# An opening with sums apart from products, and loads held back behind marks, in a fused window-attention and feed-forward kernel

## The chip, the cores and the metric

The kernel runs on one core of one Trainium2 chip. The metric is the device time of one execution in microseconds (us), as a median of runs. Nothing else runs on the chip.

## The reference

Eight batches, eight heads, 576 tokens, head dimension 64. Each token attends to the tokens at most 32 positions away. The attention's output, heads side by side, goes through a feed-forward layer with a leaky ReLU. Inputs and output are float32.

```python
scores = q @ k.T / sqrt(64)                       # per batch and head
scores = where(abs(pos_q - pos_k) <= 32, scores, -1e9)
attn = softmax(scores)
x = (attn @ v), heads side by side                # 4608 tokens x 512
h = x @ w_in                                      # 512 -> 2048
g = maximum(0.01 * h, h)
out = g @ w_out                                   # 2048 -> 512
```

## The kernel before

**Units of work.** Heads go in pairs: head p and head p + 4 lie on partitions 0 to 63 and 64 to 127, so there are four pairs p. Attention is cut into 64 steps: step i is batch i // 8, half (i // 4) % 2 of its 576 tokens (288 tokens), pair i % 4. The feed-forward layer is cut into 16 halves g of 288 tokens; half g needs the four steps 4g to 4g + 3. Each half has 16 tiles `h_tile(g, f)` (128 of the 2048 hidden units, four matmuls over the 512 inputs, one for each pair c, in one PSUM bank). The output is cut into 36 tiles of 128 tokens (`o_tile`, 16 matmuls, one copy on ScalarE (ACT), one store issued from ACT's queue).

**One attention step.** `score(i)`: five matmuls of keys (block-diagonal `kbd`) against `qT` into `ps` (L242), the exponential `e` on ACT (L248), the product with a 0/1 mask on GpSimd (POOL) into `pr` (L252). `weighted(i)`: on TensorE (PE) the sums `s` (ones times `pr`, L276 and L279, or one matmul L274 where VectorE (DVE) has joined the two parts beforehand, from step 12 on), then the products `x` with the values `vbd` (L286); on DVE the reciprocal `r` of `s` (L292) and the product of `x` and `r` into `xT` (L294). `ps`, `x` and `s` have one PSUM buffer each. `xT` is what `h_tile` reads.

**Getting q, k and v in place.** SyncE (SP) issues the float32 loads (`load_qk`, `load_v`). `cast_qk` turns q and k to bf16, on POOL, or q on DVE where `nc.vector` is given. Batches 0 to 2 are then transposed by PE (`transposes`, L201, six small matmuls for one q or k into a bank of the pool `mmps`, four banks that `h_tile` and `o_tile` also use) and copied out by ACT (L209, L215); batches 3 to 7 (`BY_DMA = 3`) by DMA transposes that SP issues (`transpose_dma`, L187), after which ACT copies as well. `place_keys` puts keys into `kbd` on DVE (L227). `cast_v` puts values into `vbd`, on POOL, or on ACT for pairs 1 to 3 of batch 0.

**Order.** Everything is ordered by hand; each engine runs its instructions in the order in which the program issues them. The opening (L427 to L488) does batch 0 and the feed-forward halves 0 and 1: step by step `score(i + 1)`, some idle matmuls (`keep_busy`, which multiply the mask and are read by nobody), `weighted(i)`; after the first four steps the 16 tiles of g = 0 with steps 5 to 7 between them; then the 16 tiles of g = 1, with the transposes of batch 1 after every fourth tile. `step()` does one later step: `score(i + 2)`, `weighted(i)`, and casts, transposes and loads for the batches to come by the table `PLAN`. From L493 on a list of `h_tile` and `o_tile` pieces is walked with a planned clock, and `spend` calls `step()` when a step's due time has come; the output tiles of half g = 1 come first.

**Loads.** The weights are loaded and cast by DMAs that POOL issues, w_in in four chunks of two DMAs each (`load_w_in`, L412; one per head row a), w_out in four chunks (`load_w_out`, L418). A load can be held back by a *mark*: a DMA of one element, from a tile that is written late into the buffer that is to be loaded, issued first (L70, L81). Batch 1's q and k stand behind a mark on w_in's second chunk (L459), its v behind a mark on w_out's second chunk (L473). Batch 2's q and k are issued without a mark, one pair before each of the steps 8 to 11 (L524).

Of the kernel before, what the change touches and what calls it, by code (L numbers as in the profile page):

```python
# [16 lines left out]
def kernel(  # L17
# [12 lines left out]
    nc = tc.nc  # L30
# [18 lines left out]
    cast = ctx.enter_context(tc.tile_pool(name="cast", bufs=1))  # L49
    attn = ctx.enter_context(tc.tile_pool(name="attn", bufs=2))  # L50
    kt = ctx.enter_context(tc.tile_pool(name="kt", bufs=4))
    prob = ctx.enter_context(tc.tile_pool(name="prob", bufs=4))
    tdma = ctx.enter_context(tc.tile_pool(name="tdma", bufs=1))
    outp = ctx.enter_context(tc.tile_pool(name="outp", bufs=4))
    PS = bass.MemoryType.PSUM
# [68 lines left out]
    nc.vector.memset(kbd[0], 0.0)  # L124
    clear(vbd[0], 0)
    clear(vbd[0], 1)

# [8 lines left out]
    for lo in (0, 64):  # L138
        w = win[lo:lo + 64]
        nc.gpsimd.affine_select(  # L140
            out=w, in_=w, compare_op=ALU.is_ge, fill=0.0,
            base=0, channel_multiplier=-1, pattern=[[0, 3], [1, 128]],
        )
        nc.gpsimd.affine_select(
            out=w, in_=w, compare_op=ALU.is_ge, fill=0.0,
            base=2 * W, channel_multiplier=1, pattern=[[0, 3], [-1, 128]],
        )
    win_f = win.rearrange("p n c -> p (n c)")
    mask = [const.tile([128, NCOL], BF16, name=f"mask{i}") for i in range(2)]

# [27 lines left out]
                nc.gpsimd.tensor_copy(out=vbd[b % 2][r, p, :, r], in_=vf[b, p][r])  # L178


    BY_DMA = 3
    qkT, asked = {}, {}

    def transpose_dma(b, p):
        for which, src in (("q", qb), ("k", kb)):
            t = tdma.tile([128, RUN, 96], BF16, name=f"{which}T{p}")
            nc.sync.dma_start_transpose(out=t, in_=src[:, p].rearrange("p c a d -> p (c a d)"))  # L187
            qkT[b, p, which] = t
        asked[b, p] = state["done"]

    def transposes(b):

# [44 lines left out]
    def score(i):  # L237
        b, hf, p = where(i)
        ps = scps.tile([128, 1024], FP32, name="ps")
        c0 = 512 - HALF  # L240
        for blk, q0, n in WIN[hf]:
            nc.tensor.matmul(  # L242
                ps[:, c0:c0 + n], kbd[b % 2][:, p, blk],
                qT[b][:, p, q0:q0 + n], start=True, stop=True,
            )
            c0 += n
        e = attn.tile([128, NCOL], BF16, name="e")
        nc.scalar.activation(  # L248
            out=e, in_=ps[:, 512 - HALF:512 - HALF + NCOL], func=AF.Exp, scale=scale,
        )  # L250
        pr = prob.tile([128, NCOL], BF16, name="pr")
        nc.gpsimd.tensor_mul(pr, e, mask[hf])  # L252
        probs[i] = pr, None

    def join(i):


        hf = where(i)[1]
        pr = probs[i][0]
        both = prob.tile([128, HALF], BF16, name="both")  # L260
        o0 = ODD[hf]
        o1 = o0 + NCOL - HALF
        nc.vector.tensor_add(both[:, o0:o1], pr[:, o0:o1], pr[:, HALF:NCOL])  # L263
        rest = slice(0, o0) if o0 else slice(o1, HALF)
        nc.vector.tensor_copy(out=both[:, rest], in_=pr[:, rest])  # L265
        probs[i] = pr, both

    def weighted(i):
        b, hf, p = where(i)
        pr, both = probs.pop(i)  # L270
        x = xps.tile([128, HALF], FP32, name="x")
        s = xps.tile([128, HALF], FP32, name="s")
        if both is not None:
            nc.tensor.matmul(s, ones_bd, both, start=True, stop=True)  # L274
        else:
            nc.tensor.matmul(  # L276
                s, ones_bd, pr[:, 0:HALF], start=True, stop=False, skip_group_check=True,
            )
            nc.tensor.matmul(  # L279
                s[:, ODD[hf]:ODD[hf] + NCOL - HALF], ones_bd, pr[:, HALF:NCOL],  # L280
                start=False, stop=True, skip_group_check=True,
            )
        c0 = 0
        for n_, (blk, q0, n) in enumerate(WIN[hf]):
            a = q0 - HALF * hf
            nc.tensor.matmul(  # L286
                x[:, a:a + n], vbd[b % 2][:, p, blk, :], pr[:, c0:c0 + n],
                start=(n_ == 0), stop=(n_ == len(WIN[hf]) - 1), skip_group_check=True,
            )
            c0 += n  # L290
        r = attn.tile([128, HALF], FP32, name="r")
        nc.vector.reciprocal(r, s)  # L292
        t0 = (b * S + hf * HALF) % RING
        nc.vector.tensor_mul(xT[:, p, t0:t0 + HALF], x, r)  # L294

    gT = const.tile([128, FFC, RING], BF16)

    def h_tile(g, f):  # L300

        t0 = g * HALF % RING
        h = mmps.tile([128, 512], FP32, name="mm", tag="mm")
        for c in range(DMC):
            nc.tensor.matmul(  # L305
                h[:, 0:HALF], w_in_bf[:, c, ts(f, 128)], xT[:, c, ds(t0, HALF)],
                start=(c == 0), stop=(c == DMC - 1),
            )
        nc.scalar.activation(  # L309
            out=gT[:, f, ds(t0, HALF)], in_=h[:, 0:HALF], func=AF.Prelu, alpha=0.01,  # L310
        )

    def o_tile(j, hook=None):

# [46 lines left out]
    def step():  # L361
# [7 lines left out]
        if b > 0:  # L369
            upto = 8 * (b + 1) + (PLAN[b > 1][0][r] if b + 1 < BY_DMA else 0)  # L370
            step_transposes(max(upto - 1, 8 * (b + 1)))
        if i < 7:
            score(i + 1)
        elif 8 <= i < NC - 2:
            nb, _, np_ = where(i + 2)
            if nb >= BY_DMA:
                step_transposes(8 * nb + 2 * np_ + 2)
                place_keys()
            score(i + 2)
# [2 lines left out]
        if b > 0:  # L382
            step_transposes(upto)
        if 0 < b < B - 1:
            for p in PLAN[b > 1][1][r] if b + 1 <= BY_DMA else ():
                cast_qk(b + 1, p)
                if b + 1 == BY_DMA:
                    transpose_dma(b + 1, p)
                if b + 2 < B:
                    load_qk(b + 2, p)  # L390

            n, p = (b + 1, 3) if r == 0 else (b + 2, r - 4)
            if p in range(4 if r == 0 else 3) and BY_DMA < n < B:
                step_transposes(8 * (n - 1) + 2 * p + 2)
                place_keys()
                cast_qk(n, p)
                transpose_dma(n, p)
                if n + 1 < B:
                    load_qk(n + 1, p)
# [7 lines left out]
    w_in_r = moe_w_in.rearrange("(a u d) f -> a d u f", a=2, d=D)  # L407
    w_out_r = moe_w_out.rearrange("(c p) f -> p c f", p=128)

    def load_w_in(f0, f1):  # L410
        for a in range(2):
            nc.gpsimd.dma_start(  # L412
                out=w_in_bf[64 * a:64 * a + 64, :, f0:f1], in_=w_in_r[a, :, :, f0:f1],
            )
# [14 lines left out]
    cast_qk(0, 1, nc.vector)  # L429
    first_pair()  # L430
    first_pair()
    clear(vbd[0], 2)
    cast_v(0, 0)
    cast_qk(0, 2, nc.vector)
    score(0)
    load_w_in(0, 512)
    first_pair()
    clear(vbd[0], 3)
    cast_qk(0, 3, nc.vector)
    load_w_in(512, 1024)  # L440
    for i in range(NPAIR):
        score(i + 1)
        if i + 1 < NPAIR:
            cast_v(0, i + 1, on_act=True)
        if i < 2:
            load_w_in(1024 + 512 * i, 1536 + 512 * i)
        else:
            load_w_out(i - 2)
        if i > 0:
            keep_busy(3 if i == 1 else 2)  # L450
        weighted(i)
        if i == 0:
            first_pair()
    state["done"] = NPAIR

    for p in range(NPAIR):
        load_qk(1, p, w_in_bf[0:1, 0, 512:514] if p == 0 else None)  # L459
    keep_busy(2)  # L460
    step()
    load_w_out(2)
    load_w_out(3)
    for f in range(FFC):
        h_tile(0, f)
        if f in (2, 6, 10):
            step()
        if f % 4 == 3:
            nc.gpsimd.memset(kbd[1][:, f // 4], 0.0)
    cast_qk(1, 0, nc.vector)  # L470
    cast_qk(1, 1, nc.vector)
    for p in range(NPAIR):
        load_v(1, p, w_out_bf[0:1, 4, 0:2] if p == 0 else None)  # L473
    second = transposes(1)
    for f in range(FFC):
        h_tile(1, f)
        if f % 4 == 3:
            p = f // 4
            next(second)
            next(second)  # L480
            place_keys()
            if p + 2 < NPAIR:
                cast_qk(1, p + 2, nc.vector)
            nc.gpsimd.memset(vbd[1][:, p], 0.0)  # L484
        if f == 11:
            score(8)
    state["tp"] = 16
    score(9)  # L488

# [11 lines left out]
    for us, kind, g, f in plan:  # L503
        if kind == "h" and f == 0:
            at[g] = t
        t += us
    due = []
    for i in range(8, NC):
        prev = 0.9 * O_US * 4 if i < 12 else at[i // 4 - 1] - LEAD
        due.append(prev + (at[i // 4] - LEAD + (1.2 if i < 12 else 0) - prev) * (i % 4 + 1) / 4)  # L510
    clock = 0.0
    cast_v(1, 0)
    turn = 0

    def spend(us):
        nonlocal clock, turn
        while due and due[0] <= clock:
            due.pop(0)
            i = state["done"]
            if i < 11:  # L520
                cast_v(1, i - 7)

            if i < 12:
                load_qk(2, i - 8)  # L524
            step()
            if 10 <= i < 14:
                load_v(2, i - 10)

        b, p = state["tp"] // 8, state["tp"] % 8 // 2
        turn += 1  # L530
        if kind == "o" and turn % 2 and b >= BY_DMA and (b, p, "k") in qkT and state["done"] > asked[b, p] + 2:
            step_transposes(state["tp"] + 1)
            place_keys()
        clock += us
# [35 lines left out]
```

## Time and profile before

| what | value |
|---|---|
| median of 3 runs | 328.59 us (328.4 to 329.43) |
| the profiled execution | 329.43 us, span 327.72 us |
| PE busy | 305.5 us, 2463 matmuls |
| DVE busy | 225.9 us |
| ACT busy | 223.6 us |
| POOL busy | 180.3 us |
| DMA transposes issued by SP | 40 |
| HBM read, written | 36.70 MB, 9.44 MB |
| granted TensorE clock | 1.0 |

The profile is of one execution. Busy times are of the span, which starts with the first instruction that the profiler holds and ends with the last; the time of the execution is 1.71 us longer. A busy PE is one with a matmul in flight, and matmuls overlap, so group means of matmuls are longer than their spacing. In lines of the timeline the columns are start, duration (both us), engine, line of the kernel, operation, what it writes and reads, and in brackets how long the engine was idle before and who released it; "SPq" and "ACTq" are those engines' queues when they issue a DMA. In a line of stages the columns are the stage, its length, and busy time with the number of instructions for PE, weight loads (PEld), DVE, ACT and POOL, then the granted clock, the DMA engines' mean share (transfers in flight on one engine can overlap, so it can exceed 1) and GB/s. In lines of DMA queues the columns are packets, MB and the time that the packets took as a share of the sixteen DMA engines' time.

### The profile page before, as it was taken

Reading aid. Unit: us, or ns where it says so; the run is one execution under the profiler, and the core shown is the slowest. Engines: PE = TensorE matmul, PEld = TensorE weight load, DVE = VectorE, ACT = ScalarE, POOL = GpSimd, SP = SyncE. Lnnn points to the kernel's source line nnn. Section 1 sums busy time; section 2 is a strip of 40 time slices with the busy share of each in tenths; the row PEclk is TensorE's granted clock in tenths of the full one; section 3 lists DMA queues with packets and bytes.
Section 4 is the critical chain, followed back from the end, with each engine's and each line's share of the span. In section 5 each row is a group of like instructions: output and inputs, shape, how many; then the busy total and the mean of one; then the engine's idle time right before and its main releaser. Section 6 shows DMA issues by size and latency. Waiting matters only on the chain.

```text
span 327.7 us, 6571 instructions
## 1 busy us (share of the span) xinstructions
PE 305.5 (93%) x2463; PEld 205.2 (63%) x2485; DVE 225.9 (69%) x310; ACT 223.6 (68%) x432; POOL 180.3 (55%) x213
## 2 busy tenths in 40 slices
PE   2578999689999999999999999999999999999996
PEld 1446784358585675758585666667675767666653
DVE  5489744587874997779776988689758867565200
ACT  6775791349385898878787878878786656555541
POOL 7798747566775596519841597339642545131000
PEclk9999999999999999999999999999999999999999
DMA  8999979968999999945997199916831001010102
GB/s 187 223 200 206 269 187 207 241 156 190 239 171 198 228 173 238 218 137 128 203 236 131 66 167 245 226 71 92 185 80 65 34 12 55 0 66 0 67 11 85
DMA packets 85172, 48.28 MB, mean 147 GB/s; under 512 B 64020, under 2 KB 80660, under 8 KB 85140
## 3 DMA queue, kind: packets, MB, share of 16 engines
q1 hardware_dynamic: 75524, 34.22, 55.6%
q10 hardware_dynamic: 5328, 9.44, 8.5%
q0 software_dynamic: 4288, 4.20, 7.9%
q8 instruction: 19, 0.31, 0.4%
q14 instruction: 13, 0.11, 0.1%
HBM read 36.70 MB, written 9.44 MB: 141 GB/s over the span
## 4 chain that ended last, share of the span: by engine, by line
PE 78%; DMA 10%; DVE 3%; POOL 3%; SPq 2%; issue 2%; ACT 1%; ACTq 0%; DVEq 0%; POOLq 0%
PE mm L305 34%; PE mm L322 33%; DMA kf<-in_k_dram 10%; PE x L286 4%; PE ps L242 4%; DVE r L292 2%; PE s L274 2%; SPq L72 1%; SPq L83 1%; POOL pr L252 1%; POOL vbd L484 1%; PE tp L201 1%; DVE xT L294 1%; POOL kb L168 1%; POOL vbd L178 0%
## 5 line engine op out<-in xcount | busy, mean ns | idle before, releaser
L292 DVE RECIPROCAL r<-s 128x288 f32<-128x288 f32 x64 | 125.1, 1954 | 35.7 <-PE s L274 26.1
L252 POOL TENSOR_TENSOR pr<-e,mask 128x544 bf16<-128x544 bf16 x64 | 77.9, 1218 | 103.2 <-ACT e L248 83.3
L305 PE MATMUL mm<-xT,w_in_bf 128*128 128x288 bf16 x1024 | 133.1, 286 | 0.0
L322 PE MATMUL mm<-w_out_bf,gT 128*128 128x512 bf16 (+2 forms) x571 | 128.3, 373 | 1.1
L309 ACT ACTIVATE gT<-mm 128x288 bf16<-128x288 f32 x256 | 101.3, 414 | 22.1 <-PE mm L305 9.4
L305 PEld LDWEIGHTS <-w_in_bf 128*128 128x128 bf16 x1024 | 98.3, 98 | 23.9
L322 PEld LDWEIGHTS <-gT 128*128 128x128 bf16 x592 | 56.4, 98 | 59.8
L248 ACT ACTIVATE e<-ps 128x544 bf16<-128x544 f32 x64 | 40.0, 624 | 26.3 <-ACT o_sb L327 5.7
L327 ACT ACTIVATE o_sb<-mm 128x512 f32<-128x512 f32 (+2 forms) x37 | 21.7, 586 | 45.8 <-PE mm L322 45.8
L227 DVE COPY kbd<-kT 64x576 bf16<-64x576 bf16 x64 | 28.6, 447 | 28.8 <-ACT kT L215 28.2
L178 POOL CAST vbd<-vf 64x576 bf16<-64x576 f32 x58 | 38.7, 668 | 1.9
L294 DVE TENSOR_TENSOR xT<-x,r 128x288 bf16<-128x288 f32 x64 | 29.3, 458 | 6.7
L168 POOL CAST kb<-kf 96x768 bf16<-96x768 f32 x32 | 27.3, 854 | 9.8 <-DMA kf<-in_k_dram 9.8
L242 PE MATMUL ps<-qT,kbd 128*128 128x128 bf16 (+2 forms) x320 | 26.8, 216 | 3.1 <-ACT e L248 3.1
L242 PEld LDWEIGHTS <-kbd 128*128 128x128 bf16 x320 | 20.9, 101 | 11.6 <-issue 3.6
L286 PE MATMUL x<-pr,vbd 128*128 128x128 bf16 (+2 forms) x320 | 26.3, 214 | 1.8 <-DVE xT L294 1.3
L263 DVE TENSOR_TENSOR both<-pr 128x256 bf16<-128x256 bf16 x52 | 23.5, 452 | 3.4 <-POOL pr L252 2.5
L286 PEld LDWEIGHTS <-vbd 128*128 128x128 bf16 x320 | 20.8, 99 | 6.6 <-DVE xT L294 2.1
L209 ACT ACTIVATE qT<-qT 128x576 bf16<-128x576 bf16 x20 | 23.6, 1179 | 1.2 <-ACT o_sb L327 1.2
L215 ACT ACTIVATE kT<-kT 128x576 bf16<-128x576 bf16 x20 | 23.5, 1177 | 0.0
L265 DVE COPY both<-pr 128x32 bf16<-128x32 bf16 x52 | 21.1, 405 | 0.0
L168 POOL CAST qb<-qf 96x768 bf16<-96x768 f32 x24 | 19.7, 821 | 0.0
(39 smaller groups left out, 110.2 us busy)
## 6 DMA issues: line engine op xcount, KB each, us to landing
qf<-in_q_dram SPq DMA_DIRECT2D x32, 288.0 KB, 4.7
kf<-in_k_dram SPq DMA_DIRECT2D x32, 288.0 KB, 5.4
vf<-in_v_dram SPq DMA_DIRECT2D x64, 144.0 KB, 5.1
out_dram<-o_sb ACTq DMA_DIRECT2D x35, 256.0 KB, 2.1
w_in_bf<-in_moe_w_in_dram POOLq DMA_DIRECT2D x8, 256.0 KB, 6.4
w_out_bf<-in_moe_w_out_dram POOLq DMA_DIRECT2D x4, 512.0 KB, 14.0
qT<-qb SPq DMA_TRANSPOSE x20, 4.9
kT<-kb SPq DMA_TRANSPOSE x20, 4.2
```

Of the source, the lines that this page charges most:

```text
L168: eng.tensor_copy(out=dst[:, p], in_=src[b, p].rearrange("p a (c d) -> p c a d", d=D),)
L178: nc.gpsimd.tensor_copy(out=vbd[b % 2][r, p, :, r], in_=vf[b, p][r])
L227: nc.vector.tensor_copy(out=kbd[b % 2][r, p, :, r], in_=kT[r].rearrange("p (n j) -> p n j", j=64),)
L242: nc.tensor.matmul(ps[:, c0:c0 + n], kbd[b % 2][:, p, blk], qT[b][:, p, q0:q0 + n], start=True, stop=True,)
L248: nc.scalar.activation(out=e, in_=ps[:, 512 - HALF:512 - HALF + NCOL], func=AF.Exp, scale=scale,)
L252: nc.gpsimd.tensor_mul(pr, e, mask[hf])
L286: nc.tensor.matmul(x[:, a:a + n], vbd[b % 2][:, p, blk, :], pr[:, c0:c0 + n], start=(n_ == 0), stop=(n_ == len(WIN[hf]) - 1), skip_group_c ...
L292: nc.vector.reciprocal(r, s)
L294: nc.vector.tensor_mul(xT[:, p, t0:t0 + HALF], x, r)
L305: nc.tensor.matmul(h[:, 0:HALF], w_in_bf[:, c, ts(f, 128)], xT[:, c, ds(t0, HALF)], start=(c == 0), stop=(c == DMC - 1),)
L309: nc.scalar.activation(out=gT[:, f, ds(t0, HALF)], in_=h[:, 0:HALF], func=AF.Prelu, alpha=0.01,)
L322: nc.tensor.matmul(o[:, lo:hi], gT[:, f, ds(128 * j % RING, 128)], w_out_bf[:, f, lo:hi], start=(f == 0), stop=(f == FFC - 1),)
```

## The change

- `weighted` is split into `sums` (matmuls into `s`, and the reciprocal), `product` (matmuls into `x`) and `scaled` (the product into `xT`). In the opening they are issued apart: a step's sums may come before the transposes of another pair, its product after. `keep_busy` is no longer called.
- `h_first(g, hooks)` issues the first four tiles of a half pair by pair over four PSUM banks: for each pair c, the matmuls of the four tiles. For g = 0 attention work stands as hooks before the pairs c = 2 and c = 3.
- The first chunk of w_in is issued one head row at a time; the order of casts, clears and weight loads in the opening is another.
- Batch 1's q and k stand behind a mark on w_out's first chunk; its v follows without a mark. Three of the four transposes of batch 1's pairs, and the scores of steps 8 and 9, move from half g = 1 into the output tiles that follow it, with due times of their own.
- Each of batch 2's loads stands behind a mark on the `xT` that the step before it has written.
- `BY_DMA = 4`: batch 3 is transposed by PE, batches 4 to 7 by DMA.

```diff
-    prob = ctx.enter_context(tc.tile_pool(name="prob", bufs=4))
+    prob = ctx.enter_context(tc.tile_pool(name="prob", bufs=6))
+    joined = ctx.enter_context(tc.tile_pool(name="joined", bufs=2))
+    recip = ctx.enter_context(tc.tile_pool(name="recip", bufs=3))
...
+    clear(vbd[0], 2)
...
+    nc.gpsimd.memset(vbd[0][:, 3], 0.0)
...
-    BY_DMA = 3
+    BY_DMA = 4
...
+    def h_first(g, hooks):
+        hs = [mmps.tile([128, 512], FP32, name="mm", tag="mm") for _ in range(4)]
         for c in range(DMC):
+            if c in hooks:
+                hooks[c]()
+            for f in range(4):
+                h_mms(g, f, hs[f], (c,))
+        for f in range(4):
+            h_out(g, f, hs[f])
...
     first_pair()
     first_pair()
     cast_v(0, 0)
+    score(0)
     cast_qk(0, 2, nc.vector)
+    score(1)
+    load_w_in(0, 512, (0,))
+    next(first)
+    sums(0)
+    next(first)
+    product(0)
+    place_keys()
     cast_qk(0, 3, nc.vector)
+    scaled(0)
+    sums(1)
+    cast_v(0, 1, on_act=True)
+    score(2)
+    load_w_in(0, 512, (1,))
     load_w_in(512, 1024)
+    next(first)
+    next(first)
+    place_keys()
+    product(1)
+    scaled(1)
+    cast_v(0, 2, on_act=True)
+    load_w_in(1024, 1536)
+    sums(2)
+    score(3)
+    load_w_in(1536, 2048)
+
+    def before_2():
+        product(2)
+        scaled(2)
+        cast_v(0, 3, on_act=True)
+        sums(3)
+        score(4)
+        load_w_out(0)
+
+    def before_3():
+        product(3)
+        scaled(3)
+        sums(4)
+        score(5)
+        load_w_out(1)
+
+    state["done"] = NPAIR
+
+    def second_half():
+        i = state["done"]
         weighted(i)
+        if i < 7:
+            sums(i + 1)
+        if i < 6:
+            score(i + 2)
+        state["done"] += 1
+
+    h_first(0, {2: before_2, 3: before_3})
     load_w_out(2)
     load_w_out(3)
+    for p in range(NPAIR):
+        load_qk(1, p, w_out_bf[0:1, 0, 0:2] if p == 0 else None)
+    for p in range(NPAIR):
+        load_v(1, p)
+    second_half()
+    for f in range(4, FFC):
         h_tile(0, f)
+        if f in (7, 11):
+            second_half()
...
     cast_qk(1, 0, nc.vector)
     cast_qk(1, 1, nc.vector)
     second = transposes(1)
...
+    second_half()
+    h_first(1, {})
+    for f in range(4, FFC):
         h_tile(1, f)
+        if f == 13:
+            second_pair(0)
...
+    due = [
+        (0.0, lambda: score(8)), (1.0, lambda: second_pair(1)), (2.6, lambda: second_pair(2)),
+        (3.2, lambda: score(9)), (4.4, lambda: second_pair(3)),
+    ]
+    due += [(6.0 + 1.9 * n, step) for n in range(NPAIR)]
...
+            step()
+            mark = place(i)[0:1, 0:2]
             if i < 12:
-                load_qk(2, i - 8)
-            step()
+                load_qk(2, i - 8, mark)
             if 10 <= i < 14:
-                load_v(2, i - 10)
+                load_v(2, i - 10, mark)
```

## The prediction

> **What bounds the kernel now.** I read the page first, for who is busy and where; then the busy table by stages, for where PE is not; then the chain and the timeline of the bad stages; then the DMA view of short windows, because the DMA engines turn out to set the opening. The page's busy line and slices:
>
> ```profile
> PE 305.5 (93%) x2463; PEld 205.2 (63%) x2485; DVE 225.9 (69%) x310; ACT 223.6 (68%) x432; POOL 180.3 (55%) x213
> ...
> PE   2578999689999999999999999999999999999996
> ...
> DMA  8999979968999999945997199916831001010102
> ```
>
> PE is the bound, except in the first nine slices of 8.2 us, where DMA is full. The stages say how much is missing:
>
> ```profile
> 0.00:20.00 20.00, 9.62 (x79) 6.76 (x81) 10.85 (x21) 14.54 (x20) 15.34 (x29) 1.00 1.09 203
> 20.00:48.00 28.00, 25.23 (x256) 19.19 (x254) 21.64 (x24) 20.20 (x47) 20.31 (x23) 1.00 1.09 219
> 48.00:71.00 23.00, 18.19 (x127) 9.50 (x127) 11.93 (x13) 7.11 (x13) 15.03 (x17) 1.00 1.03 214
> 71.00:324.00 253.00, 251.77 (x2001) 169.25 (x2020) 181.52 (x254) 181.18 (x354) 129.58 (x146) 1.00 0.64 130
> ```
>
> The second figure is PE's. From 71 us on only 1.2 us are idle in 253, so every PE instruction added there is paid in full and nothing removed elsewhere there gains. Idle before: 10.4 us up to 20, 2.8 up to 48, 4.8 up to 71 (while g = 1's output tiles run). The timeline shows what costs the last 4.8 us: output stores that wait on ACT's queue with the next exponentials behind them.
>
> ```profile
> 56.62 0.37 ACTq L328 DMA_DIRECT2D out_dram<-o_sb  x1
> 57.10 0.62 ACT L248 ACTIVATE e<-ps 128x544 bf16<-128x544 f32 x1 [4.55 <-PE mm L322]
> ...
> 62.03 0.34 ACTq L328 DMA_DIRECT2D out_dram<-o_sb  x1
> 62.48 0.62 ACT L248 ACTIVATE e<-ps 128x544 bf16<-128x544 f32 x1 [4.27 <-DMA kf<-in_k_dram]
> ```
>
> Now the opening's loads. SP's timeline and two 5 us windows of the DMA view (25:30, then 30:35; q0 carries the weights, q1 the fp32 loads):
>
> ```profile
> 22.72 0.73 SPq L70 DMA_DIRECT2D qf<-w_in_bf  x1
> 27.31 0.33 SPq L72 DMA_DIRECT2D qf<-in_q_dram  x1
> ```
>
> ```profile
> q0 software_dynamic: 930, 0.91, 119.2%
> ...
> q1 hardware_dynamic: 2, 0.00, 0.1%
> ```
>
> ```profile
> q0 software_dynamic: 662, 0.65, 77.7%
> q1 hardware_dynamic: 429, 0.62, 39.7%
> ```
>
> The one-element mark was issued at 22.72, and q of batch 1 could follow only at 27.31: 4.6 us. Then q1 moved nothing until 30. Single issues in the same view: pair 0's q issued 27.31, pair 1's q (28.23) landed 9.3 us later, at 37.5. A load behind a mark costs 15 us while weights stream.
>
> **Part by part.**
>
> *Batch 3's transposes return to PE.* Eight groups of six; the chain has them at 0.26 us each on the saturated path ("PE tp L201 x6"), so +2.1 us with no cover. Their PSUM tiles come from the four mm banks; ACT empties one in 0.65 us, and batch 2's groups (75 to 91 us) show no PE wait for one: 0, at worst 8 × 0.65 = 5.2. The removed DMA transposes gain nothing: no PE wait in the list of waits is for them, and ACT's copies, 1.18 us from SBUF against 0.65 from PSUM, were hidden.
>
> *Edits at nothing.* keep_busy's nine matmuls stood where PE waits anyway (the last two at 25.07, and PE then waits for DVE until 26.73). vbd's fourth clear moves to POOL, 1.05 us from 4.1, ahead of the cast of k at 5.32 that waits for its DMA. More buffers for pr, both and r: nothing waited for one.
>
> *The opening up to the first w_in matmul*, by row durations; e(i), pr(i), xT(i) are step i's exponential, masked weights and result. The exponential of step 0 no longer stands behind a clear (1.15): it runs 10.5–11.1; pr(0) 11.2–12.4 (POOL 1.2), the cast of k for pair 2 to 13.3, pr(1) to 14.5, and w_in's first head is issued at 14.5. sums(0) 12.8–13.4, reciprocal to 15.35 (1.95), keys of pair 2 (0.91) to 16.3, so score(2) 16.3–16.95, e(2) to 17.6, pr(2) 17.65–18.9. Only then does POOL issue the second head of w_in's first chunk: 18.9 against some 14.7 before. The first head is through by 18.4 (0.26 MB at the 0.20 MB/us that q0 moves alone), so the weight queue is empty for some 2 us. This second head lands 2.1 (an unloaded 256 KB store) to 5.9 us (the same piece issued at 18.9 before) after issue; nothing is queued, so 3.5: 22.4. h_first starts there, with product(2) and sums(3) behind it on PE, and DVE's chain slips: reciprocal 3 runs 25.6–27.6 (before 24.7–26.7), and at 2.4–2.8 us a step xT(7) would come at 39.5–40 (before 37.6). PE, from about 31.1: 12 tiles of four matmuls at 0.1225 (from 3.43 for 28) 5.9, three steps of 0.72, one product 0.24, 12 matmuls of h_first(1) 1.5: it asks for xT(7) at 41.0.
>
> *Batch 1 behind w_out's first chunk.* Weights resume at about 21.0; 7 pieces × 1.3 us → 30.1, w_out's first chunk 2.6 → 32.7, landing 0.9 later as the earlier pieces did: 33.6. pr(4) ends near 28.6, so its issue is in time, and the other chunks are issued (31.4–33.8) before the mark. From there mark and q up to q(1,1): loaded as before 4.6 + 10.2 (27.31 to 37.5) = 14.8 → 48.4; unloaded 1.6 (the shortest store) + 5.9 (first issue 0.81 to the second q's landing at 6.7) = 7.5 → 41.1. At 33.6 there are 1.57 MB of w_out left, 7.9 us, so it is nearer to loaded but the tail runs alone: I take 45.0, one half of the way and a little.
>
> Who waits? The casts cast_qk(1, 0) and cast_qk(1, 1) stand on DVE *ahead of* xT(7), the scaled(7) of the last second_half(). DVE is in order, so xT(7) = 45.0 + 0.56 + 0.46 + 0.1 = 46.1, and h_first(1)'s fourth group, then all of g = 1, wait from 41.0: 5.1 us of new idle. That is the step that decides.
>
> *From there to g = 2.* 46.1 + 0.5 + 12 tiles 5.9 + one transpose pair 0.5 = 53.0. Output tiles 64 × 0.216 = 13.8, scores 6 × 0.24, sums 4 × 0.24, products 4 × 0.24, three transpose pairs 3 × 0.52: 18.7 → 71.7. The stores no longer queue behind batch 2's loads, and by POOL's order vf's casts come with 2–5 us to spare, so I add only 0.3 for xT(11): 72.0. Before, g = 2 started at 71.22 (the timeline's first L305 of that stage), with step 12 (0.24+0.12+0.24) already done: +0.8 + 0.6.
>
> *Batch 2 behind its steps.* Eight marks on SP, each holding the queue 1.6–4.6 us; DMA is free by then (its share is 0.54 in 70–80). Pair 0's mark follows xT(8) at about 64, so q and k are there by 64 + 4.6 + 5 = 73.6, and the cast is asked for in step 12 at about 74. Covered, barely; uncovered it is 2–4 us once.
>
> **Sum:** 0.8 + 0.6 + 2.1 = +3.5. The profiled execution took 329.43 (span 327.72), 0.84 over the median 328.59, so 332.9 as profiled, **332.1** by the median. With q(1,1) at its ends, 41.1 and 48.4: 328.2 and 335.5.
>
> **Two rules weighed against rows.** Row: q1 moved 0.00 MB in 25–30 with q issued at 27.31. The Trainium skill ("DMA: Bandwidth & Descriptors", "Queues, rings and completion order") says that a DMA engine goes round robin between queues packet by packet. By it mark and q would share at once and q(1,1) land near the unloaded end, for some 328. The row before 30 disagrees; the rows after it (0.65 and 0.62) agree.
>
> Row: five-matmul score groups take 0.65 us at 17.20 and 0.40 from 22.61, while the granted clock reads 1.00 throughout. The skill ("TensorE: Matmul & The Clock Gate", "What's actually happening") says that an idle window of about 3.4 us halves PE's clock until it has been busy as long again. By it a 5 us stall would add about 1.7 us, for 333.8; this speaks against removing the filler. My sum leaves it out.
>
> **Rivals.**
> 1. *Faster: q(1,1) lands before 40.0.* Then DVE's casts cost nothing, h(1)'s fourth group starts at 41.0, 5.1 us earlier: −1.6, so 327.0; with w_in's head at 2.1 as well, 325.5. It decides when mark plus q take under 6.4 us from 33.6. For it: w_out might yield sooner than w_in did; the 4.8 us of 48–71 go for certain. Against it: both rows of 4.6 and 10.2.
> 2. *A wash:* q(1,1) at 41–43 eats exactly what the output stage gains: 328 to 329.5.
> 3. *Slower still:* the stall is as modelled and batch 2's marks leave PE waiting for keys, or PSUM banks bind at the transposes: 332.1 + 3 = 335.
> 4. *The change doesn't do what it says:* g = 0's first tiles wait for the second half of their weights rather than for xT, so splitting sums from products gains nothing there. I expect just that (22.4 against a product that could start at 20.9); its price, 1.5 us, is in the sum.
>
> **Numbers.** Main case 0.60 (its own range 329.6 to 335.5), rival 1 0.23, rival 2 0.10, rival 3 0.07. This kernel's measurement can tell about 0.3%, ±1.0 us, from no change. Faster 0.23, same 0.10, slower 0.67. The range reaches into rival 1 and up to the loaded end: 326.6 to 335.5.
>
> **What would show it.** In the profile after: the first w_in matmul near 22.4; w_out's first chunk landing near 33.6; a PE idle of about 5 us in h_first(1), its releaser DVE xT, and before it DVE waiting for DMA qf; no ACT wait of 4 us behind a store at 48–72; g = 2 from about 72; eight more transpose groups of six between 91 and 130 us. It is wrong if PE runs through h_first(1) without a wait, or if a wait over 1 us appears past 75 us.

## The result and the profile after

The changed kernel takes 353.9 us (median of 4 runs, 352.49 to 355.16); the kernel before took 328.54 beside it (328.4 to 329.43). The ratio is 1.0765, with a 95% interval of 1.0719 to 1.081: 25.4 us slower. The profiled execution took 355.16 us (span 353.5, mean granted clock 0.966). The prediction said 332.1 us, with a range up to 335.5: the sign is right, the size is far off.

The page's lines that answer to those shown of before:

```profile
PE 313.5 (89%) x2503; PEld 210.6 (60%) x2524; DVE 229.5 (65%) x310; ACT 218.9 (62%) x431; POOL 181.4 (51%) x214
...
PE   2557929999893699999999999999999999999996
...
DMA  8999999036377984997299926993682101010102
```

PE's idle time went from 22.2 us (327.7 − 305.5) to 40.0 (353.5 − 313.5), and its busy time up by 8.0. Where, by stages (length, then PE, PEld, DVE, ACT, POOL, granted clock, DMA share, GB/s):

```profile
0.00:20.00 20.00, 8.93 (x78) 6.13 (x79) 13.12 (x20) 13.02 (x18) 15.15 (x27) 1.00 1.07 189
20.00:48.00 28.00, 18.47 (x143) 13.56 (x142) 14.90 (x15) 11.52 (x25) 19.00 (x22) 0.92 1.12 179
48.00:71.00 23.00, 18.46 (x146) 12.01 (x148) 5.36 (x12) 12.49 (x28) 9.12 (x11) 0.80 0.69 123
71.00:100.00 29.00, 27.29 (x242) 17.97 (x242) 24.43 (x31) 16.41 (x34) 19.84 (x24) 1.00 0.51 136
100.00:130.00 30.00, 21.13 (x161) 13.84 (x161) 14.99 (x22) 11.46 (x26) 13.34 (x16) 0.83 0.94 200
```

Two stages stand out. In 20 to 71 PE issues 289 matmuls where it issued 383 before, and the granted clock falls to 0.92 and 0.80 where it was 1.00. In 100 to 130, inside the stretch that before was full to within 1.2 us, 8.9 us are now idle, at a granted clock of 0.83. The list of PE's waits names them (total, times, longest, in us):

```profile
PE tp L204 <- POOL qb L172: 8.8, 1, 8.8
PE mm L327 <- DVE xT L313: 7.8, 3, 6.9
...
PE mm L327 <- DMA w_in_bf<-in_moe_w_in_dram: 3.8, 1, 3.8
```

**The wait for xT** is the one that the prediction built its sum on. The timeline shows it arise from DVE's order:

```profile
47.87 0.56 DVE L172 CAST qb<-qf 96x768 bf16<-96x768 f32 x1 [5.11 <-DMA qf<-in_q_dram]
50.35 0.56 DVE L172 CAST qb<-qf 96x768 bf16<-96x768 f32 x1 [1.93 <-DMA qf<-in_q_dram]
50.83 0.45 DVE L313 TENSOR_TENSOR xT<-x,r 128x288 bf16<-128x288 f32 x1
51.33 8.41 PE L327 MATMUL mm<-xT,w_in_bf 128*128 128x288 bf16 x44 [6.94 <-DVE xT L313]
```

DVE sits idle in front of two casts whose data is late. The 0.45 us that PE needs is behind them. And the 44 matmuls after the wait are slow: PE comes to its next instruction at 59.57, 8.2 us after 51.33, where 44 at the 0.1225 us that each takes elsewhere make 5.4. The wait costs 6.9 and then 2.9 more. In the profile's window from 51 to 57 the granted clock is 0.50; from 58 on it is 1.00.

**The wait for POOL** was not foreseen. SP's queue and the engines around it:

```profile
92.78 0.63 SPq L83 DMA_DIRECT2D vf<-xT  x1
95.97 1.36 SPq L85 DMA_DIRECT2D vf<-in_v_dram  x2
...
99.00 0.64 SPq L83 DMA_DIRECT2D vf<-xT  x1
102.94 1.61 SPq L85 DMA_DIRECT2D vf<-in_v_dram  x2
...
104.65 0.57 SPq L74 DMA_DIRECT2D qf<-in_q_dram  x1
...
106.79 0.66 SPq L83 DMA_DIRECT2D vf<-xT  x1
...
111.38 1.31 SPq L85 DMA_DIRECT2D vf<-in_v_dram  x2
...
114.69 1.47 POOL L182 CAST vbd<-vf 64x576 bf16<-64x576 f32 x2 [6.74 <-DMA vf<-in_v_dram]
...
117.39 0.82 POOL L172 CAST qb<-qf 96x768 bf16<-96x768 f32 x1
...
118.27 0.66 PE L204 MATMUL tp<-ident,qb 96*128 96x96 bf16 x6 [8.77 <-POOL qb L172]
118.73 4.24 PE L327 MATMUL mm<-xT,w_in_bf 128*128 128x288 bf16 x20
```

The last of batch 2's loads of v is at the end of a chain. Its mark (106.79) stands in SP's queue behind four loads of batch 3, the load itself cannot be issued before 111.38, 4.6 us later, POOL waits 6.7 us for it, and behind POOL's cast of v stands the cast of batch 3's q that PE wants to transpose. The two marks for v before it had held the queue as well, from 92.78 to 95.97 and from 99.00 to 102.94. In all the eight marks held it for some 24 us between 74 and 111. Batch 3 is on PE's path only because `BY_DMA` is 4 now. The six transposes and twenty matmuls after the wait occupy PE from 118.27 to 122.81, 4.5 us, against 2.7 at 0.26 for the six and 0.1225 for each of the others: another 1.8. The granted clock from 118 to 122 is 0.50.

**The opening's loads.** The second head of w_in's first chunk and w_out's first chunk:

```profile
19.62 3.11 POOL L449 DMA_DIRECT2D w_in_bf<-in_moe_w_in_dram  x5
...
25.04 2.08 PE L327 MATMUL mm<-xT,w_in_bf 128*128 128x288 bf16 x8 [3.77 <-DMA w_in_bf<-in_moe_w_in_dram]
...
30.44 0.82 POOL L455 DMA_DIRECT2D w_out_bf<-in_moe_w_out_dram  x1
...
37.60 0.73 SPq L72 DMA_DIRECT2D qf<-w_out_bf  x1
42.14 0.34 SPq L74 DMA_DIRECT2D qf<-in_q_dram  x1
```

The mark could be issued at 37.60, when w_out's first chunk had landed, and it held SP for 4.5 us, as the mark before did (4.6). Two windows of the DMA view, 38:42 and 44:46:

```profile
q0 software_dynamic: 805, 0.80, 120.6%
q1 hardware_dynamic: 2, 0.00, 0.1%
```

```profile
q1 hardware_dynamic: 335, 0.48, 90.1%
q0 software_dynamic: 75, 0.07, 20.8%
```

In 38:42 SP had issued only the mark, so q1 had nothing else to move. The load issued at 42.14 moves its first packets after 43.5; in 44:46 the weights run out and q1 has most of the DMA engines' time.

### The profile page after: what moved, and what is told of

It reads as the page before. It is cut to its first block, busy times and chain, and to the rows that moved or that the text cites. A ratio compares the mean times of both kernels' runs of the same rounds, so it can differ in the third digit from the quotient of the medians.

```text
span 353.5 us, 6671 instructions
## 1 busy us (share of the span) xinstructions
PE 313.5 (89%) x2503; PEld 210.6 (60%) x2524; DVE 229.5 (65%) x310; ACT 218.9 (62%) x431; POOL 181.4 (51%) x214
## 4 chain that ended last, share of the span: by engine, by line
PE 67%; DMA 11%; DVE 6%; issue 5%; POOL 4%; ACT 3%; SPq 2%; ACTq 0%; DVEq 0%; POOLq 0%
PE mm L327 29%; PE mm L363 28%; PE ps L245 4%; PE x L298 3%; DMA qf<-in_q_dram 3%; DMA kf<-in_k_dram 3%; DVE r L287 3%; POOL pr L255 2%; PE tp L204 2%; DMA out_dram<-o_sb 2%; DMA w_in_bf<-in_moe_w_in_dram 1%; PE s L277 1%; DVE kbd L230 1%; DMA vf<-xT 1%; DMA qf<-w_out_bf 1%
## 5 line engine op out<-in xcount | busy, mean ns | idle before, releaser
L327 PE MATMUL mm<-xT,w_in_bf 128*128 128x288 bf16 x1024 | 141.2, 295 | 11.6 <-DVE xT L313 7.8
L327 PEld LDWEIGHTS <-w_in_bf 128*128 128x128 bf16 x1024 | 101.5, 101 | 40.4 <-issue 12.5
L333 ACT ACTIVATE gT<-mm 128x288 bf16<-128x288 f32 x256 | 100.8, 414 | 32.0 <-PE mm L327 20.1
L268 DVE COPY both<-pr 128x32 bf16<-128x32 bf16 x52 | 23.6, 454 | 0.0
L204 PE MATMUL tp<-ident,qb 96*128 96x96 bf16 x96 | 7.9, 228 | 16.3 <-POOL qb L172 8.8
L212 ACT ACTIVATE qT<-qT 128x576 bf16<-128x576 bf16 x16 | 18.9, 1182 | 0.9 <-ACT o_sb L368 0.8
```

Source lines behind the costliest of these rows:

```text
L327: nc.tensor.matmul(h[:, 0:HALF], w_in_bf[:, c, ts(f, 128)], xT[:, c, ds(g * HALF % RING, HALF)], start=(c == 0), stop=(c == DMC - 1),)
L333: nc.scalar.activation(out=gT[:, f, ds(g * HALF % RING, HALF)], in_=h[:, 0:HALF], func=AF.Prelu, alpha=0.01,)
```

## The experiments

In all twelve kernels PE transposes every batch (`BY_DMA = 8`, no DMA transposes). Two are the bases: **b8** is the kernel before, **a8** the changed kernel. That takes the number of transposes out of the comparison, so their distance holds the rest of the change, with batch 3 on PE in both. The time of the kernel before, run beside each, was 328.57 to 329.02 in all of them, so that differences between kernels of two groups of runs are good to some 0.5 us. Line numbers differ: `tp` is L198 in a8 and L194 in b8. Times are medians of four runs; in brackets stand the ratio to the kernel before and its 95% interval.

**b8 and a8.**

```diff
-    BY_DMA = 3        # in the changed kernel: 4
+    BY_DMA = 8
```

> The kernel before, with all eight batches transposed by PE (BY_DMA = 8, so 40 more groups of six and no DMA transposes). It is the base for changes made to the kernel before. Theory (PE is the bound from 71 us on, groups paid in full): 40 x 0.26 = 10.4 us, 339.0. Rival (PSUM banks or POOL's casts bind at the groups): more than 13 us.

> The changed kernel with BY_DMA = 8 (32 more groups). Base for what follows; its first 120 us are those of the changed kernel. Theory (PE bound later on): 353.9 + 8.3 = 362.2, and the distance to b8 is 23, 2 less than between the two originals, because both have batch 3 on PE. Rival (batch 3's transposes on PE are what makes the late v of batch 2 cost something): b8 has the same second wait, and the distance is 15 or less.

b8 took 339.35 us (ratio 1.0312, 1.029 to 1.0334), a8 362.22 (1.1013, 1.0971 to 1.1056). 40 groups of six transposes cost 10.3 to 10.8 us, 0.26 to 0.27 each, and a8's 32 groups 8.3. At that rate the 8 groups of the change make 2.1; the changed kernel with batch 3 on DMA was not run. The distance between b8 and a8 is 22.9; 25.4 − 2.1 would be 23.3. The rest of the change thus costs the same on these bases, and a8 has the same two waits, of which b8, though it asks PE for batch 3 too, has neither:

```profile
PE tp L198 <- POOL qb L172: 9.8, 1, 9.8
PE mm L321 <- DVE xT L307: 8.0, 2, 7.6
```

**a8_xt_first: step 7's xT ahead of batch 1's casts on DVE.** Nothing else moves; the casts still wait for the late loads.

```diff
+    second_half()
     cast_qk(1, 0, nc.vector)
     cast_qk(1, 1, nc.vector)
...
-    second_half()
     h_first(1, {})
```

> a8 with the last second_half() (step 7, whose xT the half g = 1 needs) issued ahead of the two casts of batch 1's q on DVE. Theory (queue order): the 6.9 us of PE idle before the fourth group of h_first(1) vanish, and with them the half-speed matmuls behind (44 in 8.4 us instead of 5.4): 7 to 10 us less than a8. Rival (the loads themselves are late): the wait comes back at the next user of batch 1's q, k or v (the transpose pair in g = 1, or the sums of step 8), and less than 3 us go.

354.53 us (1.0783, 1.076 to 1.0806): −7.7. The wait for xT is gone from the list, and in 20 to 48 PE is busy 22.28 us instead of a8's 17.12, at a clock of 1.00. The other wait is untouched:

```profile
PE tp L198 <- POOL qb L172: 9.0, 1, 9.0
```

So the order on DVE alone, with the loads as late as they are, makes this part, as the theory had it.

**a8_no_marks: batch 2's loads without marks.**

```diff
             if i < 12:
-                load_qk(2, i - 8, mark)
+                load_qk(2, i - 8)
             if 10 <= i < 14:
-                load_v(2, i - 10, mark)
+                load_v(2, i - 10)
```

> a8 with batch 2's eight loads at the same places, but without the marks on xT. Theory (marks in SP's queue make v of batch 2 late, POOL waits for it with the casts of batch 3's q and k behind it, and PE's transposes wait for those): the 8.8 us of PE idle at 109-118 vanish together with 1.8 us of slow matmuls: 9 to 11 us less than a8. Rival (without marks the stores on ACT's queue collide again with batch 2's loads at the output tiles of g = 1, as before the change): 4 to 5 us come back and only 5 to 6 us go.

350.56 us (1.0659, 1.0632 to 1.0685): −11.7, a little more than the theory and twice the rival. The stage 100 to 130 is full again, at full clock; the wait for POOL is gone, and the wait for xT stays:

```profile
100.00:130.00 30.00, 29.89 (x270) 21.06 (x270) 23.34 (x32) 19.58 (x44) 18.96 (x23) 1.00 0.68 172
```

```profile
PE mm L321 <- DVE xT L307: 8.4, 2, 8.0
```

In 48 to 71 PE is busy 19.43 us without the marks and 19.64 with them: taking them away brings no loss back there.

**a8_xt_no_marks: both together.** The edits of the two kernels above.

> a8 with both: step 7's last product ahead of the casts, and batch 2's loads without marks. Theory (two separate waits): the savings add, 362.2 - 7.7 - 11.7 = 342.8, which leaves 3.5 over b8 for the opening. Rival (an earlier g = 2 runs into batch 2's loads, so that one wait hides the other): 346 or more.

344.2 us (1.0472, 1.0428 to 1.0516): −18.0, where the sum of the two is −19.4. They add up almost wholly, and the profiled run's clock is 1.0 throughout.

**a8_filler: how much of the first wait is the clock.** Thirty matmuls that nobody reads run in the wait for xT.

```diff
+    def filler():
+        t = scps.tile([128, 1024], FP32, name="ps")
+        for _ in range(30):
+            nc.tensor.matmul(t[:, 0:512], ones_bd, mask[0][:, 0:512], start=True, stop=True)
...
-    h_first(1, {})
+    h_first(1, {3: filler})
```

> a8, and 30 matmuls of 512 columns that nobody reads stand on PE just before it waits for xT(7), in the score's PSUM buffer; they take 6.5 us at full speed, less than the wait of 7.6 in a8. Theory (clock): the wait stays, but the matmuls behind it run at full speed: about 3 us less than a8's 362.2. Rival (the slow matmuls come from something else, weight loads or PSUM banks emptied late): no change within 1 us, or slower.

360.78 us (1.0978, 1.0944 to 1.1011): −1.4, half of what was expected, and since the intervals of the two kernels overlap, the time alone does not tell it from nothing. But the profile shows the effect itself. First a8, then the kernel with the filler:

```profile
50.15 7.10 PE L321 MATMUL mm<-xT,w_in_bf 128*128 128x288 bf16 x44 [7.59 <-DVE xT L307]
```

```profile
42.16 6.64 PE L547 MATMUL ps<-mask,ones_bd 128*128 128x512 bf16 x30
49.19 5.84 PE L321 MATMUL mm<-xT,w_in_bf 128*128 128x288 bf16 x44 [0.40 <-DVE xT L307]
```

The same 44 matmuls take 5.84 us when PE was kept busy before them, and 7.10 when it was not: 1.3 us. The stage 48 to 71 has a granted clock of 1.00 with the filler and 0.88 in a8. The expectation of 3 us came from the changed kernel; in a8 there was less to win, for its clock of 0.50 lasts about 3.2 us after the wait and that of the changed kernel about 5.9, though a8's wait is the longer one (7.59 against 6.94).

**a8_xt_nm_w: both head rows of w_in's first chunk issued together,** at the place of the first, on top of a8_xt_no_marks.

```diff
-    load_w_in(0, 512, (0,))
+    load_w_in(0, 512)
...
-    load_w_in(0, 512, (1,))
```

> The same, and both heads of w_in's first chunk are issued together, ahead of the mask product of step 2, as in the kernel before. Theory (the empty weight queue costs PE 2.5 us of waiting for w_in and shifts w_out's first chunk, hence batch 1, by as much): 2 to 3 us less, about 340, that is b8 to within 1 us. Rival (DVE's chain sets the opening once the weights are there, or the casts of k wait behind the two issues on POOL): less than 1 us.

341.39 us (1.0376, 1.0345 to 1.0408): −2.8. PE's wait for w_in falls from 2.9 to 0.7 us. This version is 2.0 us above b8.

**b8_marks: the marks in the kernel before.** Batch 2's loads come behind marks on the `xT` that `step()` has written; for that, the loads of q and k move from before `step()` to after it.

```diff
-            if i < 12:
-                load_qk(2, i - 8)
             step()
+            if i < 12:
+                load_qk(2, i - 8, mark)
             if 10 <= i < 14:
-                load_v(2, i - 10)
+                load_v(2, i - 10, mark)
```

> b8 (the kernel before, all transposes on PE) with batch 2's loads behind marks on xT, and nothing else. Theory (the marks alone make batch 2's v late): a wait of PE for POOL's casts of batch 3 appears at 100-115 us and the time rises by 9 to 12 us to 349-351. Rival (the marks cost only in company with the late start of g = 2): up by less than 3 us, or down, since the stores on ACT's queue no longer wait behind batch 2's loads (4.8 us of PE idle in 48-71 of the kernel before).

347.76 us (1.0575, 1.0542 to 1.0608): +8.4 over b8. b8's stages first, then those of b8_marks:

```profile
48.00:71.00 23.00, 19.90 (x149) 11.11 (x150) 13.50 (x15) 8.14 (x16) 16.60 (x19) 1.00 1.00 221
71.00:100.00 29.00, 28.84 (x268) 20.86 (x269) 21.93 (x32) 20.35 (x47) 20.57 (x25) 1.00 0.93 192
100.00:130.00 30.00, 29.89 (x260) 19.61 (x261) 23.58 (x31) 16.36 (x35) 15.64 (x18) 1.00 0.42 115
```

```profile
48.00:71.00 23.00, 22.50 (x174) 13.38 (x173) 14.73 (x19) 10.31 (x23) 18.02 (x20) 1.00 0.62 166
71.00:100.00 29.00, 22.28 (x218) 15.97 (x216) 16.76 (x24) 16.25 (x37) 13.89 (x18) 0.95 0.61 158
100.00:130.00 30.00, 26.42 (x212) 17.59 (x213) 20.71 (x26) 14.67 (x33) 16.78 (x19) 0.88 0.82 166
```

The marks do what they are for: the output tiles of g = 1 (48 to 71) gain 2.6 us of PE time. Then 71 to 130 lose 10.0, with one long wait of PE for POOL's cast of q:

```profile
PE tp L194 <- POOL qb L168: 10.3, 1, 10.3
```

So the marks bring this wait into the old opening too, where PE asks for batch 3. Marks in a kernel that leaves batch 3 to the DMA transposes were not run, so how much of the price needs `BY_DMA` above 3 is not shown.

**b8_qk_marks and a8_qk_marks: marks on q and k only.** The v loads go unmarked, otherwise as b8_marks and as a8.

```diff
             if 10 <= i < 14:
-                load_v(2, i - 10, mark)
+                load_v(2, i - 10)
```

> b8 with marks for batch 2's q and k alone; v goes without. Theory (the second wait is v's: its last mark is issued behind four loads of batch 3): the 10.3 us of PE waiting for POOL's casts go, while the stores on ACT's queue stay free of batch 2's loads as in b8_marks: 336 to 339, at or below b8. Rival (any mark holds SP's queue, and v behind it, too long): 345 or more.

> a8 with marks for batch 2's q and k alone. Theory (v's marks are the price): 9 to 12 us less than a8, as without any marks, 350 to 353. Rival (q's and k's marks hold the queue): less than 5 us.

b8_qk_marks took 342.29 us (1.0415, 1.0373 to 1.0456): +2.9 over b8 where a gain up to 3 was thought possible. That expectation failed, and the rival's 345 was not reached either: PE still waits 4.6 us for POOL's cast of q. a8_qk_marks took 355.8 us (1.0826, 1.0787 to 1.0865): −6.4 from a8, between theory and rival. Of the marks' 11.7 us in a8, v's make 6.4 and those of q and k, with v's gone, 5.3 (355.8 − 350.56). In b8_qk_marks the longest wait of SP in 71 to 110 is this one:

```profile
SPq L72 <- DMA out_dram<-o_sb: 7.7, 1, 7.7
```

By this listing, which infers who released a wait, a load on SP's queue waits for the end of an output store that ACT issued. The store took 6.8 us to land, at 88.1, and the load was issued at 88.17; the next load of v stands behind it. The two touch no common data; I suppose a completion semaphore that both share, but no run tested it.

**b8_wout: batch 1's q and k later, in the kernel before.** Their mark is on w_out's first chunk.

```diff
-        load_qk(1, p, w_in_bf[0:1, 0, 512:514] if p == 0 else None)
+        load_qk(1, p, w_out_bf[0:1, 0, 0:2] if p == 0 else None)
```

> b8 with batch 1's q and k behind a mark on w_out's first chunk (as in the changed kernel) instead of w_in's second, and nothing else. Theory (mark and loads stand behind the weights then under way; w_out's first chunk landed at 33.8, so q of pairs 0 and 1 come at about 44 and 46, where g = 1's transposes ask from 40 on): PE waits 4 to 6 us in g = 1, 343 to 346. Rival (g = 1's loss is taken out of the 4.8 us that PE waits in 48-71 anyway): less than 2 us more than b8.

340.41 us (1.0361, 1.0306 to 1.0416): +1.1 over b8, with overlapping intervals, and not the 4 to 6 of my theory, though the first load of q is issued at 36.93 instead of 27.45. g = 1 does lose: PE is busy 22.44 us in 20 to 48 instead of 25.25. But the next stage gives it back (22.57 instead of 19.90):

```profile
48.00:71.00 23.00, 22.57 (x188) 13.87 (x190) 15.04 (x18) 11.69 (x25) 18.24 (x20) 1.00 0.87 190
```

So late loads of batch 1 cost little in the old opening: the output tiles had waits of their own, which the shift removes.

**a8_xt_nm_w_win: the converse,** batch 1's mark back on w_in's second chunk in the best version.

```diff
-        load_qk(1, p, w_out_bf[0:1, 0, 0:2] if p == 0 else None)
+        load_qk(1, p, w_in_bf[0:1, 0, 512:514] if p == 0 else None)
```

> a8_xt_nm_w (step 7 first, no marks on batch 2, both heads of w_in's first chunk together), with batch 1's q and k behind w_in's second chunk again, as in the kernel before. Theory (what is left over b8 are waits for batch 1's keys, 2.8 us on PE, and q0's first bytes come some 6 us earlier): 2 to 3 us less than 341.4, 338 to 339.5, b8 or just below. Rival (loads of batch 1 now take bandwidth from w_in's and w_out's last chunks, which the tiles of g = 0 and the output tiles wait for): no less, or more.

343.91 us (1.0488, 1.0446 to 1.053): +2.5, where −2 to −3 was expected. A wait of PE for `qT` (2.3 us) appears, and PE is busy 18.96 us in 48 to 71 instead of 20.21. In this kernel the later mark is the better one.

**The account.** Of the 25.4 us, the transposes make 2.1; step 7's result behind the casts 7.7 and batch 2's marks (with batch 3 on PE) 11.7, the two together 18.0; the head rows of w_in apart 2.8; 2.0 are left. The other 0.5 are no more than groups of runs differ by. What makes these 2.0 in the rest of the opening was not taken apart. One candidate is `keep_busy`, which the new opening no longer calls: a score group takes 0.66 us at 24.94 and 0.40 only at 27.90 in a8_xt_nm_w, but 0.40 from 22.61 on in the kernel before. The new opening with idle matmuls put back was not run. Nothing that was run beats the kernel before, and no run shows a form of the new opening that beats the old one: its best is 2.0 above b8.

## Why the prediction was right or wrong

**Right: the sign, the mechanism of the first wait, and its place.** PE waits in `h_first(1)`, released by DVE's xT, with DVE waiting for q before it: 5.1 us predicted, 6.9 measured, and a8_xt_first removes it by moving one call. The transposes cost the 2.1 us of the sum, by the rate of the 40 and 32 groups. No ACT wait of 4 us behind a store is left in 48 to 72. Rival 4's point held too: g = 0's first tiles wait for the second half of their weights (3.8 us on PE); issuing the heads together gained 2.8, where the sum had 1.5.

**Wrong first, and most: the step "Batch 2 behind its steps", with "Covered, barely; uncovered it is 2–4 us once".** Measured: 8.8 us of waiting and 1.8 of slow matmuls in the profile, 11.7 by a8_no_marks. I followed pair 0's q and k to the first step that needs them and stopped there. I did not follow the other marks through their queues: v's marks stand in SP's queue with batch 3's loads between them, POOL casts v ahead of batch 3's q, and the other part of the same change makes PE ask for that q. The prediction's own listing gave a mark 1.6 to 4.6 us of SP and counted eight of them; their sum on one in-order queue, some 24 us as measured, is what I failed to carry on to batch 3. Rival 3 named the mechanism in part, with 3 us and 0.07. The sentence on what would make the prediction wrong, a wait over 1 us past 75 us, is what happened: it ends at 118.27.

**Wrong second: q(1,1) at 45.0.** It came at about 50.3, beyond the loaded end (48.4). The two durations after the mark were nearly right, 12.7 us where I had taken 11.4. What was late was the mark itself, 37.60 instead of 33.6: the second head of w_in landed 5.3 us after its issue, near the upper of the two bounds (2.1 and 5.9), though no weight piece was ahead of it, where I took 3.5; and w_out's first chunk, issued at 30.44, took 7.1 us more.

**Wrong third: the sum left the clock out.** The Trainium skill ("TensorE: Matmul & The Clock Gate", "What's actually happening") says that an idle window of about 3.4 us halves the clock until PE has been busy for as long. The rows agree on the half: after 6.9 us of waiting the granted clock is 0.50 and 44 matmuls cost 2.9 us more, after 8.8 us it is 0.50 and 26 transposes and matmuls cost 1.8 more. They do not agree on one length: the slow stretch lasts about 5.9 us in the first case, 3.8 in the second and 3.2 in a8. An estimate by the page was 1.7 us for a stall. That is near the second case and a8 (1.6 there, 50.15 to 57.09 against 5.4) and too low for the first. The prediction had left the term out with no reason but that the clock read 1.00 throughout in the kernel before. That kernel had no wait that long outside its first microseconds, so the row could not speak against the rule. And in the opening the reading does not show slow matmuls: in the changed kernel four w_in matmuls take 1.17 us at 28.27 and 0.65 at 31.01, and the clock reads 1.00 in both windows (28:30 and 30:32). The same holds for `keep_busy`, which "Edits at nothing" had at nothing: without it the new opening's matmuls are slow until about 30, where the old one's are slow until about 22. Whether that is its doing, and what it cost, no run shows.

Together: g = 2's first matmul was due at 72.0 and came at 81.5, 9.5 us late (5.3 for q(1,1), 2.9 for the clock, 1.1 for PE's wait for batch 1's keys before its score at 62.33, 0.2 that I cannot place); then 10.6 for the wait for POOL and the slow matmuls behind it. That is 20.1 of the 22.3 us between the predicted 332.9 and the profiled 355.16. Three short waits of PE, 0.40 us before 82.41, 0.98 before 92.99 and 0.17 before 97.91, make another 1.5; of the last 0.7 I know no single row.

On the other rule the rows leave it open. The Trainium skill ("DMA: Bandwidth & Descriptors", "Queues, rings and completion order") lets an engine take turns between queues packet by packet. In 38:42 q1 moved two packets while q0 moved 805, and a mark of one element took 4.5 us. SP had issued only the mark in that window, so this shows the mark's delay and not that a load was kept back; the load behind it, issued at 42.14, moved its first packets after 43.5, with q0 still busy. In the kernel before, the load issued at 27.31 moved nothing until 30, which speaks against turns, and then q0 and q1 moved 0.65 and 0.62 MB side by side, which speaks for them. So the prediction's "a load behind a mark costs 15 us" held about (12.7 here), but what holds the mark and the first packets no run shows.

## What to carry to other kernels

A held-back load is an entry in an in-order queue: follow each one, the small and late ones too, through the issuing queue, the cast behind it and what stands behind that cast, up to the first consumer that the same change has moved onto the critical path. Before a cast is placed on an engine that also makes operands for TensorE, ask what the cast waits for; here one call issued some lines earlier was worth 7.7 us. And where a wait of TensorE passes several microseconds, price the slow matmuls after it too: here 1.3 to 2.9 us each time.

## What the runs showed of the hardware

- A mark of one element is not a small thing: 4.5 us on SP behind streaming weights, and up to 4.6 us later, when the DMA engines were moving activations (106.79 to 111.38).
- By the profile's listing an SP load waited 7.7 us for an ACT output store that shares no data with it (b8_qk_marks); why is not shown.
- After a stall of 7 to 9 us the granted clock was 0.50, for about 5.9, 3.8 and 3.2 us in three cases (changed kernel at 51.33 and 118.27, a8 at 50.15).
- A 256 KB weight piece with no other ahead of it on its queue took 5.3 us to land, though the fp32 loads had only 0.06 MB left to move beside it (window 19.6:21).
- Loads issued 9.5 us later (36.93 instead of 27.45) cost 1.1 us, no more than the runs scatter, because the next stage had waits that the shift removes (b8_wout), and a load made earlier can cost 2.5 (a8_xt_nm_w_win).
